# Zero fills of the K and V cache gradients copied from HBM instead of from an SBUF tile

## The chip, the cores and the metric

The kernel runs on one core of a Trainium2 chip. The metric is the device time of one execution in microseconds; before the change three runs gave 816.66, 816.85 and 816.85, a median of 816.85 us.

## What is computed

The reference is one decode step of a small transformer layer together with its backward pass. One token `x` of width D = 448 goes through a layer norm, 16 query heads over 8 groups of K and V caches (a window of the last W = 4096 of Sk = 32768 positions, Dh = 256), an output projection with a residual, and a bilinear feed-forward part with a second residual:

```python
k = jnp.repeat(k_cache[:, :, Sk - W:, :], rep, axis=1)
v = jnp.repeat(v_cache[:, :, Sk - W:, :], rep, axis=1)
scores = jnp.einsum("bhqd,bhkd->bhqk", q, k) * (Dh ** -0.5)
p = _softmax(scores, axis=-1)
o = jnp.einsum("bhqk,bhkd->bhqd", p, v)
...
_out, _vjp = jax.vjp(_f, A_x, A_k_cache, A_v_cache, A_wq, A_wo, B_w_gate, B_w_up, B_w_down)
_grads = _vjp(grad_out)
```

The outputs are the new row and the gradients of all inputs, all in bf16. Two of the gradients have the size of the whole caches, 8 x 32768 x 256 each (134 MB): `out_2` for the K cache and `out_3` for the V cache. Only the last 4096 positions of a group have a gradient; the first 28672 are zero, and the kernel has to write these zeros. They are 14336 KB (14.68 MB) for each group and tensor, 16 such regions in all.

## The kernel before

**Two DMA queues.** The name FILL stands for SP's queue (`nc.sync`) and IO for POOL's (`nc.gpsimd`). After two rows of 0.9 KB, FILL carries nothing but the sixteen fills (line 62). Each has as its source the SBUF tile `zeros` (128 partitions x 8192 bf16, 16 KB a partition), read NZ = 7 times over by a broadcast, so that a region goes out in 7 x 128 pieces of 16 KB. They are issued one behind the other from the start, as the queue has room. IO carries every load and every other store, in program order; a load waits there until its place in SBUF is free, and what stands behind it waits too.

**SBUF.** The tile `S` has NS = 8 slots of 16 KB a partition. One slot holds the window of K or of V of one group (2048 KB). `K_SLOT` and `V_SLOT` (lines 35 and 36) say which slot each group's K and V use. V of groups 0 to 4 stays in slots 0 to 4; V of groups 5 and 6 passes through slot 6 and V of group 7 through slot 5. Beside `S` there are `Mt` (32 KB a partition, the moments of all groups in f32, later staging space), `Rt` (16 KB) and `zeros` (16 KB).

**Forward loop** (lines 347 to 374). For each group g: the loads for later groups are put on IO, then `softmax(g)`, `scores(g + 1)` and `moments(g)`. `scores` (through `products`, lines 264 to 273) transposes K on TensorE and multiplies it with q. `moments` (lines 312 to 335) scales K's rows by the probabilities on VectorE (line 318) and accumulates V^T K and the other sums on TensorE (lines 322, 325, 329). At the end of the loop the halves `woA` and `woB` of the output projection's weights are loaded into slots that the last groups have left, and then the weights of the feed-forward part.

**Middle.** Output projection, feed-forward part and their gradients, up to the gradient of q (line 453 and after).

**Backward loop** (from line 562). For each group V is transposed again and multiplied with the gradient of the output (lines 568 and 573), then 16 tiles of the windows' gradients are built by a matmul (line 602), copied to slots 5, 6, 7 and 0 of `S` by ScalarE and VectorE (lines 210 and 212, the helper `evac`), and stored by two DMAs on IO (line 607). Here V of every group is needed once more. Groups 0 to 4 find it in their slots. For groups 5, 6 and 7 it is loaded a second time, into slots 1, 2 and 3 as soon as groups 1, 2 and 3 are done with them; that is what `V_AGAIN = {5: 1, 6: 2, 7: 3}` says (lines 575 to 577). So V is loaded eleven times in all, K eight times. Beside the loop run the jobs that write the weights' gradients (`outer`, lines 470 to 477).

Of the kernel before, what the change touches and what calls it, by code (L numbers as in the profile page):

```python
# [7 lines left out]
bf16 = mybir.dt.bfloat16  # L8
# [5 lines left out]
D = 448  # L14
NI = 7
H = 16
G = 8
Dh = 256
W = 4096
T = 32  # L20
F = 1792
FC = 14
Sk = 32768
EPS = 1e-5
SCALE = 1.0 / 16.0
SLOT = T * Dh
NS = 8
NV = 5
HQ = H * Dh // 2
HF = F // 2  # L30
ZW = 8192
NZ = (Sk - W) * Dh // (128 * ZW)


K_SLOT = [5, 6, 7, 5, 6, 7, 5, 7]
V_SLOT = [0, 1, 2, 3, 4, 6, 6, 5]
V_AGAIN = {5: 1, 6: 2, 7: 3}


@with_exitstack  # L40
def kernel(
# [3 lines left out]
    V_, S_, P_ = nc.vector, nc.scalar, nc.tensor  # L45
    FILL = nc.sync
    IO = nc.gpsimd

    const = ctx.enter_context(tc.tile_pool(name="const", bufs=1))
# [4 lines left out]
    FILL.dma_start(out=x_bf[:], in_=A_x.rearrange("a b d -> (a b) d"))  # L54
    go_bf = const.tile([1, D], bf16, tag="rowb", name="go_bf")
    FILL.dma_start(out=go_bf[:], in_=grad_out.rearrange("a b d -> (a b) d"))
    zeros = const.tile([128, ZW], bf16)
    V_.memset(zeros[:], 0.0)
    for g in range(G):
        for o in (out_2, out_3):  # L60
            reg = o[0, g, 0:Sk - W, :].rearrange("s d -> (s d)").rearrange("(p n f) -> p n f", p=128, f=ZW)
            FILL.dma_start(out=reg, in_=zeros[:].unsqueeze(1).to_broadcast([128, NZ, ZW]))


    S = const.tile([128, NS, SLOT], bf16)
    Mt = const.tile([128, G, 2, 2 * Dh], f32)
    Rt = const.tile([128, SLOT], bf16)

    def slot(k):
        return S[:, k, :]  # L70

    def slot_kv(k):
        return S[:, k, :].rearrange("p (t d) -> p t d", d=Dh)

    Kw = [slot_kv(k) for k in K_SLOT]
    Vw = [slot_kv(k) for k in V_SLOT]

    def load_window(dst, cache, g):
        IO.dma_start(out=dst, in_=cache[0, g, Sk - W:, :].rearrange("(p t) d -> p t d", t=T))  # L79

    def load_K(g):
        load_window(Kw[g], A_k_cache, g)

    def load_V(g):
        load_window(Vw[g], A_v_cache, g)
# [174 lines left out]
    def products(Xw, vecT, g, out_ps):  # L260

        for q in range(8):
            tr = ps.tile([128, 4, 2, 128], bf16, tag="tr", bufs=2)
            for i in range(4):
                for dh in range(2):
                    P_.transpose(tr[:, i, dh, :], Xw[:, 4 * q + i, dh * 128:(dh + 1) * 128], ident_bf[:])  # L266
            xt = kt_buf()
            evac(xt, tr[:])
            for i in range(4):
                for dh in range(2):  # L270
                    P_.matmul(out_ps[:, 4 * q + i, :], lhsT=xt[:, i, dh, :], rhs=vecT[:, 4 * g + dh:4 * g + dh + 3:2],
                              start=(dh == 0), stop=(dh == 1))
# [6 lines left out]
    def scores(g):  # L279
        sT[g] = fps.tile([128, T, 2], f32, tag="sT", bufs=2, name="sT")  # L280
        products(Kw[g], qT, g, sT[g])

    def softmax(g):
        s = sT[g]
        pmax = small.tile([128, 2], f32, tag="pmax")
        V_.reduce_max(out=pmax[:], in_=s[:].rearrange("p t h -> p h t"), axis=AX)
        mt = ps.tile([2, 128], f32, tag="tmp", bufs=1)
        P_.transpose(mt[:], pmax[:], ident_f[:])
        gmax = small.tile([2, 1], f32, tag="gmax")
        V_.reduce_max(out=gmax[:], in_=mt[:], axis=AX)  # L290
        gd = small.tile([2, 2], f32, tag="gd")
        V_.tensor_scalar(out=gd[:], in0=ident_f[0:2, 0:2], scalar1=gmax[:, 0:1], scalar2=-SCALE, op0=ALU.mult, op1=ALU.mult)
        nb = ps.tile([128, 2], f32, tag="tmp", bufs=1)
        P_.matmul(nb[:], lhsT=ones_f[0:2, :], rhs=gd[:], start=True, stop=True)
        nbias = small.tile([128, 2], f32, tag="nbias")
        V_.tensor_copy(out=nbias[:], in_=nb[:])
        e = small.tile([128, T, 2], f32, tag="e_f")
        sums = small.tile([128, 2], f32, tag="psums")
        for h in range(2):
            S_.activation(out=e[:, :, h], in_=s[:, :, h], func=ACT.Exp, bias=nbias[:, h:h + 1], scale=SCALE, accum_out=sums[:, h:h + 1])  # L300
        rs = small.tile([128, 2], f32, tag="rsum")
        V_.reciprocal(out=rs[:], in_=total(sums[:], 2)[:])
        pf = small.tile([128, T, 2], f32, tag="p_f")
        V_.tensor_tensor(out=pf[:], in0=e[:], in1=rs[:].unsqueeze(1).to_broadcast([128, T, 2]), op=ALU.mult)
        V_.tensor_copy(out=pT_all[:, g], in_=pf[:])
        p_f[g] = pf

    def moments(g):

        K, Vv, pf = Kw[g], Vw[g], p_f[g]  # L310
        MT = fps.tile([128, 2, 2 * Dh], f32, tag="MT", name="MT")
        acc = fps.tile([128, 8], f32, tag="acc", name="acc")
        for c in range(T // 2):
            pk = pk_buf()
            for i in range(2):
                t = 2 * c + i
                for h in range(2):
                    V_.tensor_scalar(out=pk[:, i, h, :], in0=K[:, t, :], scalar1=pf[:, t, h:h + 1], scalar2=None, op0=ALU.mult)  # L318
            for i in range(2):
                t = 2 * c + i  # L320
                for hf in range(2):
                    P_.matmul(MT[:, hf, :], lhsT=Vv[:, t, hf * 128:(hf + 1) * 128], rhs=pk[:, i, :, :].rearrange("p h d -> p (h d)"),  # L322
                              start=(t == 0), stop=(t == T - 1))
                for hf in range(2):
                    P_.matmul(acc[:, 2 * hf:2 * hf + 2], lhsT=Vv[:, t, hf * 128:(hf + 1) * 128], rhs=pT_all[:, g, t, :],  # L325
                              start=(t == 0 and hf == 0), stop=(t == T - 1), skip_group_check=True)
                for h in range(2):
                    for dk in range(2):
                        P_.matmul(acc[:, 4 + 2 * h + dk:5 + 2 * h + dk], lhsT=pk[:, i, h, dk * 128:(dk + 1) * 128], rhs=ones_bf[:, 0:1],  # L329
                                  start=False, stop=(t == T - 1), skip_group_check=True)  # L330
        S_.copy(out=Mt[:, g, 0, :], in_=MT[:, 0, :])  # L331
        V_.tensor_copy(out=Mt[:, g, 1, :], in_=MT[:, 1, :])
        V_.tensor_copy(out=oT_f[:, 4 * g:4 * g + 4].rearrange("p (h f) -> p f h", f=2), in_=acc[:, 0:4].rearrange("p (f h) -> p f h", h=2))
        V_.tensor_copy(out=kbar[:, 4 * g:4 * g + 4], in_=acc[:, 4:8])
        V_.tensor_copy(out=oT_bf[:, 4 * g:4 * g + 4], in_=oT_f[:, 4 * g:4 * g + 4])

    wo_v = A_wo.rearrange("(b p) n -> p b n", p=128)
    woA = S[:, 6, 0:16 * D].rearrange("p (b n) -> p b n", n=D)
    woB = S[:, 5, 0:16 * D].rearrange("p (b n) -> p b n", n=D)
    wg_sb = S[:, 7, 0:NI * HF]  # L340
    wu_sb = Rt[:, 0:NI * HF]
    bc2 = [S[:, 7, NI * HF:NI * HF + F].rearrange("p (i c) -> p i c", i=2), Rt[:, NI * HF:NI * HF + F].rearrange("p (i c) -> p i c", i=2)]
# [6 lines left out]
    for g in range(G):  # L349
        if g + 1 < NV:  # L350
            load_V(g + 1)
        if g + 2 < 7:
            load_K(g + 2)
        if g == 5:
            load_V(5)
        if g == 6:
            load_V(6)
            load_K(7)
        if g == 7:
            load_V(7)  # L360
            IO.dma_start(out=woA, in_=wo_v[:, 0:16, :])
        softmax(g)
        if g + 1 < G and g != 6:
            scores(g + 1)
        moments(g)
        if g == 6:
            scores(7)
        if g == 0:

            t = ps.tile([128, D], f32, tag="tmp", bufs=1)  # L370
            P_.matmul(t[:], lhsT=ones_bf[0:1, :], rhs=go_bf[:], start=True, stop=True)
            S_.copy(out=dh2_bc[:], in_=t[:])
            for c in range(FC):
                V_.tensor_tensor_reduce(out=wd0[:, c, :], in0=wd0[:, c, :], in1=dh2_bc[:], scale=1.0, scalar=0.0,
                                        op0=ALU.mult, op1=ALU.add, accum_out=d_hh[:, c:c + 1])
# [184 lines left out]
    for g in range(G):  # L560
        if g in V_AGAIN:
            Vw[g] = slot_kv(V_AGAIN[g])
        dp = bps.tile([128, T, 2], f32, tag="dp")
        for q in range(8):
# [6 lines left out]
            for i in range(4):  # L571
                for dh in range(2):
                    P_.matmul(dp[:, 4 * q + i, :], lhsT=xt[:, i, dh, :], rhs=doT[:, 4 * g + dh:4 * g + dh + 3:2],  # L573
                              start=(dh == 0), stop=(dh == 1))
        for again, sl in V_AGAIN.items():
            if sl == g:
                load_window(slot_kv(sl), A_v_cache, again)
# [19 lines left out]
        for c in range(T // 2):  # L597
            d_ps = bps.tile([128, 2, 2, Dh], f32, tag="d2", bufs=2)
            for i in range(2):
                t = 2 * c + i  # L600
# [39 lines left out]
```

## Time and profile before

| what | before |
|---|---|
| median of the runs | 816.85 us |
| the profiled execution: its own time | 816.48 us |
| its span, first to last instruction | 814.7 us |
| instructions | 12155 |
| bytes moved by DMA | 338.66 MB |
| SP's queue (q1) | 234.88 MB |
| POOL's queue (q0) | 103.00 MB |
| the last store on POOL's queue is issued at | 761.9 us |

In the profile, q1 is SP's queue and q0 POOL's. The page cuts the span into 40 equal slices; in the strip, a digit is the busy share of a slice in tenths, the DMA row is the mean busy share of the core's 16 DMA engines, and the GB/s row is what they moved. In the list of queues the last column is the time that a queue's packets took, as a share of 16 engines' time. The strip and the list can also be had for any stretch of the span, with the packets of that stretch alone; all times in the span count from its first instruction.

### The profile page before, as it was taken

The page shows a single profiled execution, that of the slowest core. Times are in us where ns is not written, and L with a number is a line of the kernel's source. Part 1 is how long each engine was busy: PE and PEld are TensorE (multiplying, and loading weights), DVE is VectorE, ACT ScalarE, POOL GpSimd, SP SyncE. Part 2 cuts the span into 40 slices and gives each one's busy share as a digit, 9 for nine tenths or more (in the row PEclk, how much of TensorE's full clock was granted, in tenths as well). Part 3 has the DMA queues.
Part 4 walks back from the last instruction along what each step waited for, and adds up shares of the span by engine and source line. Part 5 has one row for each costly group of instructions (what it writes and reads, how often), then busy time and mean ns, then how long its engine had stood idle before and what let it go on. Part 6 is the DMA issues. An engine that isn't in the chain of part 4 may idle for free.

```text
span 814.7 us, 12155 instructions
## 1 busy us (share of the span) xinstructions
PE 504.1 (62%) x4991; PEld 301.7 (37%) x4991; DVE 374.4 (46%) x1149; ACT 165.0 (20%) x261; POOL 40.4 (5%) x75
## 2 busy tenths in 40 slices
PE   3559969999566947062995562597597848263200
PEld 3445646666434524031983421243143313010000
DVE  4128837776451644028733470754553626253200
ACT  0230211221101000001012231243343424142100
POOL 3000000000000001000001000001000010000000
PEclk9959878999785969565556555555555555555555
DMA  8999999999999999999999999999999999999993
GB/s 344 430 423 427 430 428 429 425 428 426 430 417 426 415 424 420 428 429 431 426 427 429 409 415 421 431 423 422 404 430 425 425 413 423 421 425 427 424 427 170
DMA packets 24573, 338.66 MB, mean 416 GB/s; under 512 B 1251, under 2 KB 1317, under 8 KB 4677
## 3 DMA queue, kind: packets, MB, share of 16 engines
q1 hardware_dynamic: 14596, 234.88, 68.3%
q0 software_dynamic: 9920, 103.00, 30.2%
q8 instruction: 39, 0.64, 0.3%
q14 instruction: 18, 0.14, 0.0%
HBM read 57.28 MB, written 280.59 MB: 415 GB/s over the span
## 4 chain that ended last, share of the span: by engine, by line
issue 59%; DMA 17%; PE 11%; DVE 4%; POOL 3%; ACT 1%; POOLq 0%; DVEq 0%
DMA S<-in_A_wo_dram 4%; DMA Rt<-in_A_wq_dram 4%; DMA out_dram<-Mt 3%; PE dq_ps L453 3%; DMA S<-in_A_k_cache_dram 3%; DMA S<-in_A_v_cache_dram 2%; PE MT L322 2%; POOL out_dram L477 1%; POOL S L79 1%; DVE Rt L423 1%; POOL out_dram L607 1%; PE dh_ps L159 1%; PE d_ps L602 1%; PE tr L568 1%; PE t L413 1%
## 5 line engine op out<-in xcount | busy, mean ns | idle before, releaser
L602 PE MATMUL d_ps<-R,Mt 32*128 32x512 bf16 x256 | 124.4, 612 | 94.4 <-DVE S L212 93.6
L322 PE MATMUL MT<-Rt,S 128*128 128x512 bf16 x512 | 156.8, 391 | 21.1 <-DMA S<-in_A_v_cache_dram 19.9
L318 DVE TENSOR_SCALAR Rt<-S,pf 128x256 bf16<-128x256 bf16 x512 | 117.8, 283 | 32.0 <-PE acc L329 17.3
L212 DVE CAST S<-d_ps 128x512 bf16<-128x512 f32 x128 | 86.8, 689 | 57.1 <-ACT S L210 43.9
L210 ACT CAST S<-d_ps 128x512 bf16<-128x512 f32 x128 | 75.1, 587 | 171.6 <-PE d_ps L602 171.6
L266 PE MATMUL tr<-ident_bf,S 128*128 128x128 bf16 x512 | 52.5, 267 | 44.5 <-DMA S<-in_A_k_cache_dram 41.2
L602 PEld LDWEIGHTS <-Mt 32*128 32x128 bf16 x256 | 23.2, 113 | 148.1 <-issue 146.7
L325 PEld LDWEIGHTS <-S 128*128 128x128 bf16 x512 | 49.9, 98 | 62.7 <-issue 6.6
L568 PE MATMUL tr<-ident_bf,S 128*128 128x128 bf16 x512 | 68.8, 304 | 3.5 <-ACT Mt L210 3.5
L329 PE MATMUL acc<-ones_bf,Rt 128*128 128x1 bf16 x1024 | 61.8, 163 | 0.0
L568 PEld LDWEIGHTS <-S 128*128 128x128 bf16 x512 | 48.5, 135 | 28.0 <-issue 27.8
L266 PEld LDWEIGHTS <-S 128*128 128x128 bf16 x512 | 41.4, 121 | 42.9 <-DMA S<-in_A_k_cache_dram 41.7
L210 ACT COPY Rt<-tr 128x1024 bf16<-128x1024 bf16 x32 | 32.4, 1012 | 84.7 <-PE tr L266 84.3
L325 PE MATMUL acc<-pT_all,S 128*128 128x2 bf16 x512 | 49.1, 165 | 0.0
L329 PEld LDWEIGHTS <-Rt 128*128 128x128 bf16 x1024 | 44.5, 96 | 0.0
L212 DVE COPY Rt<-tr 128x1024 bf16<-128x1024 bf16 x32 | 22.1, 690 | 48.5 <-PE tr L266 47.0
L210 ACT COPY Mt<-tr 128x1024 bf16<-128x1024 bf16 x32 | 32.4, 1014 | 56.3 <-PE tr L568 29.2
L322 PEld LDWEIGHTS <-S 128*128 128x128 bf16 x512 | 32.0, 97 | 21.7 <-DMA S<-in_A_v_cache_dram 20.4
L331 ACT COPY Mt<-MT 128x512 f32<-128x512 f32 x8 | 4.7, 586 | 164.8 <-PE MT L322 145.4
L573 PEld LDWEIGHTS <-Mt 128*128 128x128 bf16 x512 | 19.9, 108 | 36.7 <-DVE Mt L212 13.7
L573 PE MATMUL dp<-doT,Mt 128*128 128x2 bf16 x512 | 22.6, 168 | 12.3 <-DVE Mt L212 10.5
L212 DVE COPY Mt<-tr 128x1024 bf16<-128x1024 bf16 x32 | 22.0, 686 | 16.4 <-PE tr L568 11.3
(182 smaller groups left out, 435.1 us busy)
## 6 DMA issues: line engine op xcount, KB each, us to landing
out_dram<-zeros SPq DMA_DIRECT2D x16, 14336.0 KB, 149.7
out_dram<-S POOLq DMA_DIRECT2D x16, 2048.0 KB, 29.5
S<-in_A_v_cache_dram POOLq DMA_DIRECT2D x11, 2048.0 KB, 35.6
S<-in_A_k_cache_dram POOLq DMA_DIRECT2D x8, 2048.0 KB, 28.0
out_dram<-Mt POOLq DMA_DIRECT2D x6, 896.0 KB, 22.3
S<-in_A_wq_dram POOLq DMA_DIRECT2D x1, 3584.0 KB, 14.7
S<-in_A_wo_dram POOLq DMA_DIRECT2D x2, 1792.0 KB, 35.4
out_dram<-Mt POOLq DMA_DIRECT2D x3, 1024.0 KB, 35.7
```

Source lines behind the costliest of these rows:

```text
L79: IO.dma_start(out=dst, in_=cache[0, g, Sk - W:, :].rearrange("(p t) d -> p t d", t=T))
L210: S_.copy(out=out, in_=in_)
L212: V_.tensor_copy(out=out, in_=in_)
L266: P_.transpose(tr[:, i, dh, :], Xw[:, 4 * q + i, dh * 128:(dh + 1) * 128], ident_bf[:])
L318: V_.tensor_scalar(out=pk[:, i, h, :], in0=K[:, t, :], scalar1=pf[:, t, h:h + 1], scalar2=None, op0=ALU.mult)
L322: P_.matmul(MT[:, hf, :], lhsT=Vv[:, t, hf * 128:(hf + 1) * 128], rhs=pk[:, i, :, :].rearrange("p h d -> p (h d)"), start=(t == 0), stop=( ...
L325: P_.matmul(acc[:, 2 * hf:2 * hf + 2], lhsT=Vv[:, t, hf * 128:(hf + 1) * 128], rhs=pT_all[:, g, t, :], start=(t == 0 and hf == 0), stop=(t ...
L329: P_.matmul(acc[:, 4 + 2 * h + dk:5 + 2 * h + dk], lhsT=pk[:, i, h, dk * 128:(dk + 1) * 128], rhs=ones_bf[:, 0:1], start=False, stop=(t == ...
L453: P_.matmul(dq_ps[:, 2 * h + dk:2 * h + dk + 1], lhsT=Mt[:, h // 2, hf, c0:c0 + 128], rhs=doT_f[:, 2 * h + hf:2 * h + hf + 1], start=(hf = ...
L568: P_.transpose(tr[:, i, dh, :], Vw[g][:, 4 * q + i, dh * 128:(dh + 1) * 128], ident_bf[:])
L573: P_.matmul(dp[:, 4 * q + i, :], lhsT=xt[:, i, dh, :], rhs=doT[:, 4 * g + dh:4 * g + dh + 3:2], start=(dh == 0), stop=(dh == 1))
L602: P_.matmul(d_ps[:, i, :, :].rearrange("p w d -> p (w d)"), lhsT=rows[32 * k:32 * k + 32, a, :], rhs=R[32 * k:32 * k + 32, :], start=True, ...
```

## The change

The tile `zeros` is gone as a tile of its own; `S` has a ninth slot in its place, and the zeros lie in that slot at first. Only the first region of `out_2` and of `out_3` is filled from it. Each of the other fourteen regions is copied from HBM: from the whole first region of the other tensor, which holds zeros by then. The source's pieces are taken in another order than the destination's ("(n p f)" and "(p n f)"); both have pieces of 8192 elements, 16 KB.

When the two fills from SBUF are done, slot 8 takes V of group 5, and keeps it for the backward loop. V of group 5 is loaded one group earlier than before (through NV = 6), V of group 6 too; V of group 7 goes to slot 6 after group 6's moments, in two halves. `woA` and `woB` change places. `V_AGAIN` has only groups 6 and 7 left, in slots 1 and 2.

```diff
-NS = 8
-NV = 5
+NS = 9
+NV = 6
...
-V_SLOT = [0, 1, 2, 3, 4, 6, 6, 5]
-V_AGAIN = {5: 1, 6: 2, 7: 3}
+V_SLOT = [0, 1, 2, 3, 4, 8, 6, 6]
+V_AGAIN = {6: 1, 7: 2}
...
-    zeros = const.tile([128, ZW], bf16)
-    V_.memset(zeros[:], 0.0)
-    for g in range(G):
-        for o in (out_2, out_3):
-            reg = o[0, g, 0:Sk - W, :].rearrange("s d -> (s d)").rearrange("(p n f) -> p n f", p=128, f=ZW)
-            FILL.dma_start(out=reg, in_=zeros[:].unsqueeze(1).to_broadcast([128, NZ, ZW]))
...
+    zeros = S[:, 8, 0:ZW]
+    V_.memset(zeros, 0.0)
+
+    def region(o, g, order):
+        return o[0, g, 0:Sk - W, :].rearrange("s d -> (s d)").rearrange(order, p=128, f=ZW)
+
+    for g in range(G):
+        for o, other in ((out_2, out_3), (out_3, out_2)):
+            if g == 0:
+                FILL.dma_start(out=region(o, g, "(p n f) -> p n f"), in_=zeros.unsqueeze(1).to_broadcast([128, NZ, ZW]))
+            else:
+                FILL.dma_start(out=region(o, g, "(p n f) -> p n f"), in_=region(other, 0, "(n p f) -> p n f"))
...
+    def load_half(dst, cache, g, t0):
+        t1 = t0 + T // 2
+        return IO.dma_start(out=dst[:, t0:t1, :], in_=cache[0, g, Sk - W:, :].rearrange("(p t) d -> p t d", t=T)[:, t0:t1, :])
...
-    woA = S[:, 6, 0:16 * D].rearrange("p (b n) -> p b n", n=D)
-    woB = S[:, 5, 0:16 * D].rearrange("p (b n) -> p b n", n=D)
+    woA = S[:, 5, 0:16 * D].rearrange("p (b n) -> p b n", n=D)
+    woB = S[:, 6, 0:16 * D].rearrange("p (b n) -> p b n", n=D)
...
         if g == 5:
-            load_V(5)
+            load_V(6)
         if g == 6:
-            load_V(6)
             load_K(7)
-        if g == 7:
-            load_V(7)
-            IO.dma_start(out=woA, in_=wo_v[:, 0:16, :])
         softmax(g)
...
         if g == 6:
+            for t0 in (0, T // 2):
+                v7 = load_half(slot_kv(V_SLOT[7]), A_v_cache, 7, t0)
+            with tc.issue_after(v7.ins):
+                IO.dma_start(out=woA, in_=wo_v[:, 0:16, :])
             scores(7)
```

## The prediction

> **What bounds the kernel now.** I read the strip of the span first, then the queues, then both queues in chosen stretches, and only then the waits of the engines.
>
> ```profile
> PE 504.1 (62%) x4991; PEld 301.7 (37%) x4991; DVE 374.4 (46%) x1149; ACT 165.0 (20%) x261; POOL 40.4 (5%) x75
> ...
> DMA  8999999999999999999999999999999999999993
> GB/s 344 430 423 427 430 428 429 425 428 426 430 417 426 415 424 420 428 429 431 426 427 429 409 415 421 431 423 422 404 430 425 425 413 423 421 425 427 424 427 170
> ...
> q1 hardware_dynamic: 14596, 234.88, 68.3%
> q0 software_dynamic: 9920, 103.00, 30.2%
> ...
> HBM read 57.28 MB, written 280.59 MB: 415 GB/s over the span
> ```
>
> No compute engine is busy for two thirds of the span, and the DMA engines are full in every slice between the first and the last. The two queues take 68.3 + 30.2 = 98.5% of the engines' time. So a wait of PE or VectorE in the middle costs nothing by itself. What counts is how many bytes the two queues carry, at what price, and how the last 50 us run empty. q1 is SP's: the sixteen fills of 14336 KB (14.68 MB). q0 is POOL's: all loads, and the stores of the windows and weight gradients.
>
> Price of a fill packet: the two queues in 356 to 380 us, where the fills are nearly alone.
>
> ```profile
> DMA packets 633, 10.31 MB, mean 430 GB/s; under 512 B 3, under 2 KB 3, under 8 KB 3
> ...
> q1 hardware_dynamic: 629, 10.27, 100.1%
> ```
>
> 629 packets, nearly all of 16 KB, in 24 us of 16 engines are 24 x 16 x 1.001 / 629 = 0.611 us each. Over the whole span q1 comes to 234.88 / (0.683 x 814.7) = 422 GB/s of its own time and q0, half of it reads of HBM, to 103.00 / (0.302 x 814.7) = 419. Reading HBM into SBUF and writing SBUF to HBM thus cost the same per byte, alone or mixed.
>
> When the first two fills are done, and how the queues share: first the stretch 0 to 131 us, then 131 to 763 us, where 763 is just after the last store is issued (761.9 in the timeline).
>
> ```profile
> q1 hardware_dynamic: 1800, 29.13, 52.0%
> q0 software_dynamic: 1878, 25.04, 46.3%
> ```
>
> ```profile
> DMA packets 19678, 267.49 MB, mean 423 GB/s; under 512 B 973, under 2 KB 1021, under 8 KB 3901
> ...
> q1 hardware_dynamic: 12089, 194.45, 73.1%
> q0 software_dynamic: 7545, 72.44, 27.3%
> ```
>
> Two fills are 29.36 MB, so they land at about 132 us. While both queues have work, q0 holds 46 to 47% (46.3 here; 47.3 in 85 to 105 us). After that q0 has only 27.3%, so both have work for 0.273 / 0.47 = 58% of the 632 us, and SP's queue is alone for the other 42%, 265 us.
>
> **The change, part by part.** The profiled execution took 816.48 us (span 814.7 and 1.8 around it), 0.4 under the median of 816.85; the sum starts from 816.5.
>
> *The zero tile in slot 8.* The same memset of 128x8192 (3.5 us from its row), the same two first fills, nothing before them on their queue: 0.
>
> *The wait on SP.* The first copy reads what the two zero fills write, so SP holds it until both have landed, at about 132 us. Before, three fills had been issued by 40 us. Behind it on SP stand only the other copies, and no engine waits for them before the end. What is lost is SP's queue running dry between landing and the first new packet: one issue (0.6 us, the shortest of the L62 issues) and a landing (the last fill packet ends 0.8 us before the closing drain). POOL's queue has 3.4 MB to move between 120 and 140 us and covers part. 0 to 3 us; I take 2.
>
> *One V load less.* V of group 5 stays in slot 8, so eleven V loads become ten: 2.10 MB / 0.423 = 5.0 us of all engines. As the DMA is full, it all counts: -5.
>
> *The moved loads.* V of group 5 is issued at group 4 (about 171 us; slot 8 has been free since 132), V of group 6 at group 5 behind it, V of group 7 in halves right after group 6's moments. On POOL each of these waits for VectorE or PE to be done with a slot, as before (235.3 us of "S L79 <- DVE Rt L318" in the waits), and behind them stand only later loads of the same phase. In the chain of waits V of group 7 is a wait of 17.7 us at 279; the first half may now come some 10 us sooner. The full DMA engines hide that: 0, and -10 at most if they stop being the bound. The exchanged places of the two halves of wo: 0, as both are issued in the same stretch (280 and 315 us) into slots freed there.
>
> *Fourteen fills become copies from HBM to HBM.* This decides. 14 x 14.68 = 205.5 MB, 14 x 896 = 12544 packets if the 16 KB pieces stay, 784 per engine, 479 us at 0.611 us each. Written bytes do not change; read bytes go from 57.3 to 57.3 + 205.5 - 2.1 = 260.7 MB. No row shows a DMA from HBM to HBM, so it is bounded by the nearest ones.
> - Lower bound: the same packet at the same 0.611 us. Reads and writes have one price and do not disturb each other in the mixed stretches, so the 430 GB/s belong to the DMA engines or the SBUF side, and HBM is not seen to bind. Cost 0. Below nothing is not excluded, if the SBUF side sets the price: copies do not touch it.
> - Upper bound: HBM gives, reads and writes together, no more than the 430 shown. Copies then cost double: +479 us, somewhat less where they share with q0.
> - Between them: lone copies would ask HBM for 2 x 427 = 854 GB/s, copies mixed half and half with q0 for 1.5 x 427 = 640, against at most 431 shown in any slice. Because mixing reads and writes at 431 raises the packet's price by nothing, I do not put the limit near 431 but nearer to the upper demand: mixed stretches keep their price, lone copies cost 1.2 times. That is an estimate, a fifth of the way from the lower bound (no rise at 431) to the upper. It gives 265 x 0.2 = +53 us.
>
> The Trainium skill, HBM Reference, section "Specifications (TRN2)", gives an HBM domain about 716 GB/s; no run here shows it, and it speaks against this change: lone copies could then not pass 358 GB/s, 1.19 times the price, and the sum would be 864 us.
>
> The opposite comes from DMA: Bandwidth & Descriptors, section "Where 436 GB/s comes from", which makes the SBUF ports the bottleneck: by that alone copies that touch no SBUF could be cheaper than fills, and the 430 GB/s above fit it without deciding it.
>
> Sum: 816.5 + 2 - 5 + 0 + 53 = 866.5 in the profiled execution, 867 as the median.
>
> **Rivals.**
> *Copies cost what fills cost* (811 to 816.5, centre 814): 816.9 - 5 + 2. For it: one price in every row. Against it: HBM would have to carry twice what it is seen to carry. It ends on the faster side; the place is the 265 us of lone copies and the switch-over point is 3 / 265: if they are dearer than 1.1%, the gain of 3 us is gone.
> *Copies are cheaper* (775 to 811): the SBUF side sets the 0.611 us and copies avoid it. At 0.9 in the lone stretches 814 - 26 = 788. It cannot go far: the last store pair is issued at 761.9, and its 4.2 MB need 10 us, so 775 at the least while compute keeps its pace. For it: identical price in both directions, both through SBUF. Against it: the same doubled HBM traffic.
> *HBM binds at what is shown* (1200 to 1292): from 132 us on 2 x 205.5 + 75.9 = 487 MB at 0.43 are 1132; 132 + 1132 and some 10 of tail are about 1275. Against it: no sign of strain at 430.
> *It does not do what it says:* copies could be cut into other pieces than 16 KB. That would show in q1's packet count, and at the small sizes that q0 carries the price per byte hardly rises (419 against 422 GB/s), so it is no case of its own.
>
> **How the numbers follow.** About 0.2%, 1.6 us, is what a measurement of this kernel can tell from no change. Lone copies at 1.05 to 2 times, with mixed stretches partly held too: 0.49, slower; its own range is 827 to 1000 us with a thin end to 1100. Equal price: 0.24, of it 0.21 faster and 0.03 within 0.2%. Cheaper: 0.12, faster. Double: 0.15, slower. That makes faster 0.33, same 0.03, slower 0.64. The forecast is 867, from the likeliest case. The range 795 to 1100 leaves out the double price (0.15) and the lower part of the cheap copies (0.05).
>
> **What would show it.** HBM read 260.7 MB, written 280.6 as before; ten V loads. A first copy on SP that waits until about 132 us. If I am right: in stretches with an idle q0 the GB/s row falls from 430 to 430 / 1.2 = 358, q1's packets rise from 0.61 to 0.73 us there, compute ends near 760 to 780 and SP then waits some 70 us or more for copies alone, where before it ended 51 us after the last store's issue together with q0. Equal GB/s in lone stretches means the first rival; more than 431, the second; 215, the third. My forecast is wrong if q1's packet stays at 0.611 us, or if the mixed stretches become dearer as well.

## The result: 894.8 us, and the profile after

| | before | after |
|---|---|---|
| median | 816.81 us (4 runs) | 894.81 us (893.0 to 896.27, 4 runs) |
| profiled execution, span | 816.48, 814.7 us | 895.45, 893.7 us |
| bytes moved, counted once | 338.66 MB | 336.56 MB |
| last store issued on POOL's queue | 761.9 us | 769.3 us |

The ratio is 1.0955 (95% interval 1.0942 to 1.0969): 78 us slower, while 2.1 MB less is moved. The page of the changed kernel, with the lines that answer to those of before:

```profile
PE 502.8 (56%) x4947; PEld 304.0 (34%) x4991; DVE 374.4 (42%) x1149; ACT 164.7 (18%) x261; POOL 40.4 (5%) x75
...
DMA  8999999999999999999999999999999999999995
GB/s 350 430 422 429 428 431 417 358 370 381 369 371 357 330 376 378 322 345 351 341 372 388 409 370 408 393 393 419 380 395 386 404 405 384 427 403 335 325 321 188
...
q1 hardware_dynamic: 14596, 234.88, 70.0%
q0 software_dynamic: 9920, 100.90, 28.6%
...
HBM read 260.70 MB, written 280.59 MB: 606 GB/s over the span
```

The engines have the same work and the DMA row the same nines, but the GB/s row under it has fallen: the copies run from 132 us on, and from the eighth slice on (156 us) all but two slices lie between 320 and 410 until the tail, where before they lay between 404 and 431. A full DMA row only says that packets are in work, not at what pace. q1 has the same 14596 packets and bytes and now holds 70.0% of a span that is 79 us longer. HBM read is the 260.7 MB that the prediction worked out.

The same kernel where SP's queue is alone, the middle part (362 to 380 us) and then the end (815 to 880 us):

```profile
DMA packets 351, 5.75 MB, mean 319 GB/s; under 512 B 0, under 2 KB 0, under 8 KB 0
...
q1 hardware_dynamic: 350, 5.73, 99.2%
```

```profile
DMA packets 1307, 21.07 MB, mean 324 GB/s; under 512 B 21, under 2 KB 21, under 8 KB 21
...
q1 hardware_dynamic: 1307, 21.07, 98.8%
```

Before, such a stretch ran at 430 GB/s. Now it is 319 and 324, with every engine busy: a 16 KB packet takes 0.82 and 0.80 us instead of 0.611, 1.34 and 1.31 times as long. Where both queues have a backlog, 780 to 800 us, the old rate is nearly there:

```profile
DMA packets 566, 8.52 MB, mean 426 GB/s; under 512 B 46, under 2 KB 46, under 8 KB 46
...
q1 hardware_dynamic: 282, 4.39, 52.2%
q0 software_dynamic: 284, 4.13, 49.0%
```

What SP waited for in the changed kernel:

```profile
SPq L72 <- DMA out_dram<-S: 128.6, 2, 66.8
SPq L644 <- DMA out_dram<-out_dram: 107.6, 2, 67.1
```

The first line is the two waits for the zero fills, the second holds the wait for the last copies at the end: POOL's queue has its last packet at 808 us, and the copies that fell behind, 24.8 MB, then run alone until 892. This is how the cost of the lone stretches appears: compute goes on at its pace, the copies lag, and the lag is paid after the last store.

### The profile page after: what moved, and what is told of

It is laid out like the page before. It is cut to its first block, busy times and chain, and to the rows that moved or that the text cites. A ratio compares the mean times of both kernels' runs of the same rounds, so it can differ in the third digit from the quotient of the medians.

```text
span 893.7 us, 12108 instructions
## 1 busy us (share of the span) xinstructions
PE 502.8 (56%) x4947; PEld 304.0 (34%) x4991; DVE 374.4 (42%) x1149; ACT 164.7 (18%) x261; POOL 40.4 (5%) x75
## 2 busy tenths in 40 slices
DMA packets 24572, 336.56 MB, mean 377 GB/s; under 512 B 1250, under 2 KB 1316, under 8 KB 4676
## 3 DMA queue, kind: packets, MB, share of 16 engines
q1 hardware_dynamic: 14596, 234.88, 70.0%
## 4 chain that ended last, share of the span: by engine, by line
issue 36%; DMA 25%; PE 13%; DVE 5%; another core or an unknown queue 4%; POOL 2%; ACT 1%; POOLq 0%; DVEq 0%
DMA S<-in_A_wo_dram 8%; DMA out_dram<-Mt 8%; DMA S<-in_A_k_cache_dram 5%; DMA Rt<-in_A_wq_dram 4%; PE dq_ps L462 3%; PE MT L331 3%; PE tr L275 1%; DVE Rt L327 1%; POOL out_dram L486 1%; DVE Rt L432 1%; POOL out_dram L616 1%; PE dh_ps L168 1%; PE ao L392 1%; PE acc L338 1%
## 5 line engine op out<-in xcount | busy, mean ns | idle before, releaser
L331 PE MATMUL MT<-Rt,S 128*128 128x512 bf16 x468 | 145.9, 388 | 2.1 <-DVE Rt L327 1.7
L219 ACT COPY Rt<-tr 128x1024 bf16<-128x1024 bf16 x32 | 32.4, 1012 | 68.4 <-PE tr L275 67.9
L392 PE MATMUL ao<-S,oT_bf 128*1 128x448 bf16 x32 | 9.0, 436 | 56.7 <-DMA S<-in_A_wo_dram 56.7
```

The lines of the kernel that those rows point to most:

```text
L219: S_.copy(out=out, in_=in_)
L392: P_.matmul(ao[:], lhsT=oT_bf[:, b:b + 1], rhs=wo_b(b), start=(b == 0), stop=(b == 31))
```

## The experiments

Three theories were set against each other. Theory 1: reads and writes of HBM have one limit together, so a copy, which uses HBM twice, is dear only where little else runs beside it. Theory 2: a copy's packet is dearer in the DMA engine itself. Theory 3: the pattern of addresses is at fault. The three kernels with DMA work alone were run once each.

**Copies alone, in stages.** Only `zeros`, the fills and copies are left of the kernel. The two first fills are followed, on SP, by:

```diff
+    FILL.dma_start(out=region(o2, 1, A), in_=region(o3, 0, B))
+    FILL.dma_start(out=region(o3, 1, A), in_=region(o2, 0, B))
+    FILL.dma_start(out=region(o2, 2, A), in_=region(o3, 0, A))
+    FILL.dma_start(out=region(o3, 2, A), in_=region(o2, 0, A))
+    FILL.dma_start(out=region(o2, 3, A), in_=region(o2, 0, B))
+    FILL.dma_start(out=region(o3, 3, A), in_=region(o3, 0, B))
+    FILL.dma_start(out=region(o2, 4, A), in_=region(o3, 0, B)[:, 0:1, :].to_broadcast([128, NZ, ZW]))
+    FILL.dma_start(out=region(o3, 4, A), in_=region(o2, 0, B)[:, 0:1, :].to_broadcast([128, NZ, ZW]))
+    FILL.dma_start(out=region(o2, 5, A), in_=zsrc())
+    FILL.dma_start(out=region(o3, 5, A), in_=zsrc())
+    FILL.dma_start(out=region(o2, 6, A, 14), in_=region(o3, 0, B, 14))
+    FILL.dma_start(out=region(o3, 6, A, 14), in_=region(o2, 0, B, 14))
+    FILL.dma_start(out=region(o2, 7, A, 8), in_=region(o3, 0, B, 8))
```

(A is "(p n f)", B is "(n p f)"; the last argument is the outer dimension, 128 where none is given.)

> Only the fills and copies, one behind the other on SP's queue, no loads, no arithmetic: two fills from SBUF, then pairs of copies (source order as in the change; source order equal to the destination's; same tensor; a 2 MB source read seven times), two fills from SBUF, two copies spread over 14 DMA engines, one over 8. Theory 1 (HBM limits reads and writes together, some 645 GB/s by the 322 GB/s of the lone copies in the changed kernel): about 322 GB/s in every pair whatever the order, 322 also with 14 engines, and 8 engines x 26.8 = 214 GB/s with 8, because 2 x 214 is far under the limit; 34.3 us for a fill, 45.6 for a copy, span about 665 us. Theory 2 (a copy packet is dearer in the engine itself, 0.611 x 1.33 = 0.81 us wherever it runs): 322 with 16 engines, 282 with 14, 161 with 8; span about 700 us. Theory 3 (the pattern of addresses costs it): the pairs differ; equal order or the other source is near 430, or the 2 MB source well under 322.

Measured: 662.04 us, span 660.3. Each stretch below lies inside one stage. The change's own order, 95 to 125 us:

```profile
DMA packets 618, 9.86 MB, mean 329 GB/s; under 512 B 16, under 2 KB 16, under 8 KB 16
```

Source in the same order as the destination, 175 to 250 us:

```profile
DMA packets 400, 25.17 MB, mean 336 GB/s; under 512 B 16, under 2 KB 16, under 8 KB 16
```

Source in the same tensor as the destination, 285 to 325 us:

```profile
DMA packets 835, 13.42 MB, mean 335 GB/s; under 512 B 16, under 2 KB 16, under 8 KB 16
```

A source of 2 MB, read seven times, 370 to 415 us:

```profile
DMA packets 941, 15.16 MB, mean 337 GB/s; under 512 B 16, under 2 KB 16, under 8 KB 16
```

Fills from SBUF, 430 to 480 us:

```profile
DMA packets 1335, 21.61 MB, mean 432 GB/s; under 512 B 16, under 2 KB 16, under 8 KB 16
```

Copies over 14 engines, 500 to 560 us:

```profile
DMA packets 1184, 19.17 MB, mean 319 GB/s; under 512 B 14, under 2 KB 14, under 8 KB 14
...
q1 hardware_dynamic: 1184, 19.17, 87.1%
```

A copy over 8 engines, 590 to 640 us:

```profile
DMA packets 663, 10.80 MB, mean 216 GB/s; under 512 B 4, under 2 KB 4, under 8 KB 4
...
q1 hardware_dynamic: 663, 10.80, 50.3%
```

Neither the source tensor nor the size of the source moves the rate (329 to 337), nor does equal order, which went as 64 KB packets of some 3.1 us, 0.78 us for 16 KB: theory 3 falls. With 14 of 16 engines (87.1% of engine time) the total stays at 319, where theory 2 had 282. With 8 engines it is 216 GB/s, and the trace has 0.611 us for every 16 KB packet, the fill's own price: theory 2, which had 161 GB/s there, falls. What stays nearly constant is the sum over the core, as theory 1 says: twice 319 to 337 is 638 to 674 GB/s of reads and writes.

**Fills beside copies, loads beside copies.** Again only DMA work. In the first, seven fills from SBUF on SP's queue run beside seven copies on ACT's:

```diff
+    for g in range(1, 8):
+        FILL.dma_start(out=region(o2, g, A), in_=zsrc())
+        nc.scalar.dma_start(out=region(o3, g, A), in_=region(o2, 0, B))
```

> Only fills and copies: after two fills, seven fills from SBUF on SP's queue run beside seven copies on ACT's queue. Theory 1: packets of both queues alternate, HBM is asked for 1.5 x 427 = 640 GB/s, just at the limit, so all 16 transfers go at some 425 GB/s, 16 x 34.3 = 550 us and a few more. Theory 2: the seven copies keep their dearer price, 9 x 34.3 + 7 x 45.6 = 628 us.

Measured: 557.09 us, span 555.3. From 100 to 500 us (q1 the fills, q10 the copies):

```profile
DMA packets 10694, 172.07 MB, mean 430 GB/s; under 512 B 192, under 2 KB 192, under 8 KB 192
...
q10 hardware_dynamic: 5399, 86.88, 51.0%
q1 hardware_dynamic: 5295, 85.18, 49.7%
```

The copies cost exactly what the fills cost, at 430 GB/s written and 217 read (86.88 MB in 400 us), 647 together. In the second, the seven copies are on SP's queue and 48 window loads on POOL's:

```diff
+    for g in range(1, 8):
+        FILL.dma_start(out=region(o3, g, A), in_=region(o2, 0, B))
+    for n in range(48):
+        cache = (A_k_cache, A_v_cache)[n % 2]
+        nc.gpsimd.dma_start(out=S[:, n % 8, :].rearrange("p (t d) -> p t d", d=Dh),
+                            in_=cache[0, (n // 2) % 8, Sk - W:, :].rearrange("(p t) d -> p t d", t=T))
```

> Only DMA work: two fills from SBUF, then seven copies on SP's queue beside 48 loads of 2 MB windows on POOL's queue. HBM is asked for two reads and one write where the run with fills beside copies asked for one read and two writes. If the limit is one on reads and writes together (some 645 GB/s): both queues at 0.611 us a 16 KB packet and 427 GB/s in sum, as there, span about (29.4 + 102.8 + 100.7) / 0.425 + 10 = 558 us. If reads are limited sooner: packets longer than 0.611 us beside the loads, sum under 427.

Measured: 562.41 us, span 560.4; from 100 to 500 us, and then 510 to 550 us, where the loads have ended:

```profile
DMA packets 11216, 171.97 MB, mean 430 GB/s; under 512 B 720, under 2 KB 720, under 8 KB 720
...
q1 hardware_dynamic: 5727, 92.26, 54.1%
q0 software_dynamic: 5489, 79.71, 46.5%
```

```profile
DMA packets 831, 13.35 MB, mean 334 GB/s; under 512 B 16, under 2 KB 16, under 8 KB 16
```

430 GB/s read and 231 written, 661 together, at the old price; the moment the copies are alone they fall to 334. So neither the reads (430 pass) nor the writes (430 pass in the run above) are limited near 330 by themselves.

These runs leave one more reading: a limit of some 330 GB/s on copies as such, whatever runs beside them. In all three tests at the old price the copies went at 231 GB/s or less. The whole kernel tells the two apart, in stretches where POOL's queue moves small packets and so holds only a quarter to a third of the engines' time. First the kernel before, 323 to 348 us, then the changed one at the same work, 320 to 349 us:

```profile
DMA packets 998, 10.67 MB, mean 427 GB/s; under 512 B 31, under 2 KB 31, under 8 KB 447
...
q1 hardware_dynamic: 502, 8.22, 77.0%
q0 software_dynamic: 496, 2.45, 23.9%
```

```profile
DMA packets 1028, 10.85 MB, mean 374 GB/s; under 512 B 46, under 2 KB 46, under 8 KB 462
...
q1 hardware_dynamic: 514, 8.18, 71.1%
q0 software_dynamic: 514, 2.68, 29.8%
```

The copies move 8.18 MB in 29 us, 282 GB/s, well under 330, and still the total falls from 427 to 374. Reads and writes together are (2 x 8.18 + 2.68) MB in 29 us, 656 GB/s. So it is the sum that is limited, somewhere from 640 to 670 GB/s. Whether the limit sits in HBM itself or on the way to it, no run tells apart.

**Half of the copies in the whole kernel.** The kernel before, its zero tile and plan for V kept, with `n` counting the fills in order:

```diff
+            n = 2 * g + (0 if o is out_2 else 1)
+            if 2 <= n < 9:
+                FILL.dma_start(out=region(o, g, "(p n f) -> p n f"), in_=region(other, 0, "(n p f) -> p n f"))
+            else:
+                FILL.dma_start(out=region(o, g, "(p n f) -> p n f"), in_=zeros[:].unsqueeze(1).to_broadcast([128, NZ, ZW]))
```

> The kernel before with its own zero tile and plan for V; only the first seven of the fourteen later fills (groups 1 to 3 and out_2 of group 4) are copies, the rest come from the zero tile. All fourteen cost some 85 us (894.8 less the 5 us saved by a V load, against 816.8). Theory 1: the price is paid where SP's queue is alone; laying a limit of 640 to 650 GB/s over the trace of before in steps of 6 us puts 59 to 64 us on the first seven: about 878 us. Theory 2: half of 85, about 859 us.

> As the run with the first seven, but the last seven fills are copies (out_3 of group 4, groups 5 to 7). Theory 1: POOL's queue is busy beside them most of the time; the same working puts 31 to 36 us on them: about 850 us, some 28 less than with the first seven. Theory 2: about 859 us, the same as with the first seven.

Measured: 856.5 us for the first seven (ratio 1.0483, 1.0465 to 1.0500), 843.2 for the last seven (1.0325, 1.0309 to 1.0340): +40.1 and +26.8 over the 816.4 of before. That seven copies cost 13 us more or less with their place speaks for theory 1, since packets dearer in themselves would give the same; but the difference is half of what was expected, and the +40 alone is nearer to theory 2's 42 than to 59 to 64. Part of the miss is the limit: these ran on the chip of the stages above, where the lone copies went at some 335 GB/s, 670 instead of 645. Laid over the packets of before in the same steps of 6 us, 670 gives about 48 and 21, an estimate. That is 8 us too high for the first seven and 6 too low for the last, and this rest is not explained. One cause is seen but not sized: the working holds POOL's queue at its old times, while in fact that queue moved 26.4 MB beside the seven copies, against 22.0 beside the same fills before, and copies are cheaper with more beside them.

**The copies without the new plan for V, and the saved load without the copies.** First all fourteen copies with the old zero tile and plan (the diff above with `if g > 0:`).

> The kernel before with its own zero tile and plan for V, and all fourteen later fills copied as in the change: the copies without the load that the change saves and without the loads that it moves. If the saved load is worth its 2.10 MB of full DMA time (4.9 us) and the moved loads nothing: 894.8 + 5 = 900 us (898 to 902). If the new plan for V was worth nothing beside the copies: 895. If the moved loads cost something: under 895.

Measured: 887.08 us (ratio 1.0864, 1.0850 to 1.0879), 7.7 under the changed kernel where 5 over it was expected. Its lone copies at the end ran at 332 to 333 GB/s by its page, against 321 to 325 in the changed kernel, so either the new plan cost 12 us or the two runs had met different conditions at HBM. Both kernels were run again, one after the other on one chip:

> The changed kernel once more, on the same chip as the run after it, because copies with the old plan for V came out 7.7 us under it where 5 us over it was expected, in another call. If that gap is a matter of the chip or the placement (lone copies went at 330 GB/s there and at 323 here): some 882 to 885 us, 5 under the old plan's 887. If the new plan for V costs 12 us beside copies: 893 to 896 again.

> Copies with the old plan for V and its own zero tile, on the same chip as the changed kernel. Chip or placement: 4 to 6 us over the changed kernel of this call. The new plan costs time: 6 to 10 us under it.

Measured: 883.77 us for the changed kernel (882.48 to 884.76; ratio 1.0822, 1.0806 to 1.0838) and 888.9 for the old plan (886.16 to 889.43; 1.0888, 1.0870 to 1.0906). Here the new plan saves 5.1 us, so the 7.7 us of the first comparison were not the plan's. The changed kernel again, 820 to 860 us:

```profile
DMA packets 811, 13.03 MB, mean 326 GB/s; under 512 B 16, under 2 KB 16, under 8 KB 16
```

and in 362 to 380 us it has 331 GB/s where the first profile had 319. Chip or placement of the tensors was not told apart, and neither is shown: the old plan took 887.1 and 888.9 us on two chips, nearly the same, and on one chip its lone copies still went 2% faster than those of the new plan (332 and 337 GB/s in the two stretches, against 326 and 331). So the 5.1 us may be what slower copies leave of a larger saving.

Then the saved load by itself, with the old fills; the kernel takes for V of group 7 what lies in its slot:

```diff
-            if sl == g:
+            if sl == g and again != 7:
                 load_window(slot_kv(sl), A_v_cache, again)
```

> The kernel before, all fills from the zero tile, but V of group 7 is not loaded again for the backward loop (it takes what lies in slot 3): ten V loads in place of eleven. It shows what the saved load would be worth with the old fills. DMA bound everywhere: 2.10 MB / 0.427 = 4.9 us less, 811.6 us. If the load were hidden: 816.5.

Measured: 811.65 us (ratio 0.9941, 0.9927 to 0.9955), 4.8 us less. The load is worth its bytes. What the change spends to save it, fourteen copies, costs 71 to 72 us (887.1 less 816.5, 888.9 less 816.6). No version that beats the kernel before came out of this. One region copied in a lone stretch costs 14.68 / 0.324 - 14.68 / 0.430 = 11 us more than a fill, an estimate from the rates above, and the load saves 5. Whether a few copies, placed only where POOL's queue has a backlog, would pay was not tried.

## Why the prediction was right, and where it was off

- *What bounds the kernel.* Right: the DMA queues do. The last store was issued only 7 us later than before, while the end came 79 us later.
- *The deciding term.* The mechanism held, in its place: copies keep their price where POOL's queue has half of the engines' time, lose part of it where that queue has less, and lose most alone. Its size failed. The step is "lone copies cost 1.2 times", a fifth of the way from no rise to double; measured 430 / 324 = 1.33 in the changed kernel, a third of the way. With 265 x 0.33 = 87 in place of 53 the sum of 866.5 becomes 900.5, 5 over the 895.45 of the profiled execution. The 265 us of lone time held. In the changed kernel the queues have these shares in 131 to 763 us:

```profile
q1 hardware_dynamic: 10605, 170.62, 72.4%
q0 software_dynamic: 7478, 67.77, 27.7%
```

  By the prediction's own working that is 0.277 / 0.47 = 59% with both queues and 41%, 260 us, of lone copies; with the 84 us from 808 to 892 it makes 344, against 265 x 1.33 = 352.
- *The reason given for 1.2* was that mixing reads and writes at 431 GB/s raised nothing, so the limit had to be far off. It was a guess between two ends: a price that does not rise says that the limit is above 431, and nothing about how far above. That the forecast came within 28 us is in part luck; the direction is not, since any rise well over 1.1% would have given it.
- The Trainium skill, *HBM Reference, "Specifications (TRN2)"*, with its 716 GB/s per domain gave 864, an estimate. The runs agree in kind; in size they reach 638 to 674 GB/s, 89 to 94% of it, and the estimate was 31 us short.
- The Trainium skill, *DMA: Bandwidth & Descriptors, "Where 436 GB/s comes from"*, with the SBUF ports as the bottleneck, would have let copies run faster than fills. The runs disagree: with 8 engines and no SBUF on either side a 16 KB packet takes the same 0.611 us.
- *The wait on SP*, 2 us: it cost nothing, and the sign given for it, a first copy that waits until about 132 us, did not show. The copy that reads `out_2` was issued first, at 68.4 us, when the first fill had landed and the second was still moving, so the queue did not run dry (431 GB/s in 130 to 136 us).
- *The V load*, -5: 4.8 without copies; with them, load and moved loads together, 5.1. *The moved loads*, 0: V of group 5 was issued at 136.4 us, sooner than the 171 that I took, after POOL had waited 28.8 us for the fills; the K load behind it went out at 145.2, before at 145.5. The halves of group 7 came at 245 and 254 instead of 279.
- *The rivals.* Equal price is refuted where copies are alone, and true where the other queue takes half of the engines' time. Cheaper copies and double price are refuted by 319 to 337 GB/s in all lone stretches.

## What to carry to other kernels

A copy from HBM to HBM is one transfer to the DMA engines and two to the memory. In these runs it cost no more than a fill where transfers that touch HBM once had half of the engines' time, an eighth of the total rate where they had 30% of it (374 GB/s instead of 427), and a third more where it was alone; so weigh where in the span it runs, not its bytes. And when a kernel's DMA row is all nines, read the GB/s row under it: the first shows that queues are full, only the second shows at what pace they empty.

## What the runs showed of the hardware that was not expected

- The medians of the kernel before agree to 0.4 us in all series (816.4 to 816.8), while the changed one was 894.8 in one series and 883.8 in another, over 1% apart. It is one case: copies with the old plan gave 887.1 and 888.9. The cause is open.
- A copy whose two sides have the same order went out in 64 KB packets, with no gain in rate (336 GB/s).
- A source of 2 MB read seven times (337 GB/s) was no slower than a source of 14.68 MB (329).
